# Five Q and K pieces instead of six, and the second V half in one PSUM bank: 32 fewer TensorE instruction pairs a segment

## The chip, the cores and the metric

One core of one Trainium2 chip. The metric is the device time of one execution in microseconds; lower is better. It is about 2 us more than the span from the first to the last instruction that the profile shows. Runs of one kernel can be disturbed and are then marked slow. A ratio in this document is the mean time of one kernel's fast runs over that of the other's of the same rounds, so it is not quite the ratio of the medians quoted beside it. The rule calls a difference under 2% "same".

## The reference, cut to what matters

A recurrent attention over 64 segments, followed by a gated MLP. Each segment takes 32 new rows and 8 memory rows, and its memory output is an input of the next segment, so the 64 segments can't overlap freely.

```python
for s in range(n_seg):                       # 64 segments
    h = jnp.concatenate([mem, xs], axis=1)   # 8 + 32 rows, width 512
    q = jnp.einsum('btd,dhe->bhte', h, Wq)   # 32 heads of 128
    k = jnp.einsum('btd,dhe->bhte', h, Wk)
    v = jnp.einsum('btd,dhe->bhte', h, Wv)
    scores = jnp.where(mask, jnp.einsum('bhqe,bhke->bhqk', q, k) * scale, -1e9)
    o = jnp.einsum('bhqk,bhke->bhqe', _softmax(scores), v)
    o = jnp.einsum('bhte,hed->btd', o, Wo)
    mem = o[:, :M, :]                        # goes into the next segment
```

## The kernel before

The kernel records every operation with what it reads and writes, and works out the semaphore waits itself. The 32 rows of a segment are the stationary operand, 32 columns wide, so four matmuls on four column tiles run side by side ("a quad" below). Work goes in two halves of 16 heads, `b` = 0 and 1. A Q or K piece is `(half, first head pair, head pairs, (bank of Q, bank of K))`; `mi` is 0 for Q, 1 for K.

```python
QKP = ((0, 0, 8, (0, 1)), (1, 0, 4, (6, 7)), (1, 4, 4, (3, 2)))
PVB = (0, 1, 6, 7)                      # banks that PV writes
VB = {(0, 0): 6, (1, 0): 2, (1, 1): 7}  # banks of V

def QK(s, piece, mi):                   # 16 matmuls: 4 quads
    b, p0, np_, banks = piece
    ...
    for dc in range(DC):
        for c in range(4):
            ...
            pe(lambda e, ...: e.matmul(ps[32*c:32*c+32, bank, 0:32*nh], lhsT=hT[:, sl, dc, :], rhs=rhs, ...))

def QK_evac(piece, mi):                 # ACT copies PSUM to Tst, DVE transposes into QT or KT
    ...
def V_evac(b, eng, gs=(0, 4)):          # a copy of V from PSUM to SBUF, on ACT or DVE
    ...
def PV_half(s, b):                      # needs V_sb and the normalised E_sb of half b
    ...

# per segment, cut
for piece in QKP:
    for mi in range(2):
        QK(s, piece, mi)
        QK_evac(piece, mi)
S_half(s, 0); sm_exp(0)
V_half(s, 0, (0, 1, 2))
S_half(s, 1)
sm_sums(0); sm_exp(1); sm_ln(0)
V_half(s, 0, (3,)); V_evac(0, "dve")
V_half(s, 1, gs=(0, 2)); V_evac(1, "dve", (0, 2))     # 16 matmuls of 256 columns, bank 2
sm_sums(1); sm_rcp(0); sm_ln(1); sm_rcp(1)
V_half(s, 1, gs=(2, 4)); V_evac(1, "act", (2, 4))     # 16 of 256 columns, bank 7
sm_norm(0); sm_norm(1)
...                                                   # filler matmuls for later segments, if any
PV_half(s, 0); PV_half(s, 1)
```

Of the kernel before, what the change touches and what calls it, by code (L numbers as in the profile page):

```python
# [169 lines left out]
def fast_path(nc, st, keep, A_x, A_mem0, A_Wq, A_Wk, A_Wv, A_Wo, A_seg_len, B_w_in, B_w_sp, B_b_sp, B_w_out, out):  # L170
# [25 lines left out]
    em = Emitter(n_dma_sems=40)  # L196
# [67 lines left out]
    def PB(b):  # L264
        return ("ps", b)
# [4 lines left out]
    def pe(fn, **k):  # L270
        return em.add("pe", fn, **k)
# [104 lines left out]
    def slot(s):  # L376
        return s % NSLOT
# [74 lines left out]



    QKP = ((0, 0, 8, (0, 1)), (1, 0, 4, (6, 7)), (1, 4, 4, (3, 2)))
    SBK = (0, 1)
    PVB = (0, 1, 6, 7)
    VB = {(0, 0): 6, (1, 0): 2, (1, 1): 7}
# [6 lines left out]
    OC = 384  # L465
    VXB = 5

    def QK(s, piece, mi):
        b, p0, np_, banks = piece
        ws = (w_q, w_k)[mi]  # L470
        bank = banks[mi]
        sl = slot(s)
        h0, nh = 16 * b + 2 * p0, 2 * np_
        for dc in range(DC):
            for c in range(4):
                rhs = ws[:, dc, :].rearrange("p (h c i) -> p c h i", c=4, i=32)[:, c, h0:h0 + nh, :]
                pe(lambda e, dc=dc, c=c, rhs=rhs: e.matmul(ps[32 * c:32 * c + 32, bank, 0:32 * nh], lhsT=hT[:, sl, dc, :], rhs=rhs,  # L477
                                                           start=(dc == 0), stop=(dc == DC - 1), tile_position=(0, 32 * c)),
                   reads=[("hTx", (s // 4) % 3), ("hTm", s), ("W", mi, 2 * b), ("W", mi, 2 * b + 1)], writes=[PB(bank)])

    def halves(b, p0, np_):
        return range(p0 // 4, (p0 + np_) // 4)

    def QK_evac(piece, mi):
        b, p0, np_, banks = piece
        bank = banks[mi]
        st_ = Tst[:, mi, 64 * p0:64 * (p0 + np_)]
        tok = [("T", mi, k) for k in halves(b, p0, np_)]
        act(lambda e: e.activation(out=st_.rearrange("p (hp i r) -> p hp i r", i=32, r=2),  # L489
                                   in_=ps[:, bank, 0:64 * np_].rearrange("p (hp r i) -> p hp i r", r=2, i=32), func=ACT.Copy),  # L490
            reads=[PB(bank)], writes=tok)
        src = st_.bitcast(U32)
        dt_, nm = ((QT, "QT"), (KT, "KT"))[mi]
        dst = dt_[:, b, p0:p0 + np_, :, :].rearrange("p hp q r -> p (hp q r)").bitcast(U32)
        if mi == 0:
            dst = dst.rearrange("p (hp q) -> p hp q", hp=np_)[:, :, 8:40]
        dve(lambda e: e.transpose(out=dst, in_=src), reads=tok, writes=[(nm, b, k) for k in halves(b, p0, np_)])  # L497
# [70 lines left out]
    def V_half(s, b, dcs=range(DC), gs=(0, 4)):  # L568
        bank = VB[b, gs[0] // 2]
        sl = slot(s)  # L570
        w = 128 * (gs[1] - gs[0])
        for dc in dcs:
            for c in range(4):
                c0 = (16 * b + 4 * c + gs[0]) * DH
                pe(lambda e, dc=dc, c=c, c0=c0: e.matmul(ps[32 * c:32 * c + 32, bank, 0:w], lhsT=hT[:, sl, dc, :], rhs=w_v[:, dc, c0:c0 + w],  # L575
                                                         start=(dc == 0), stop=(dc == DC - 1), tile_position=(0, 32 * c)),
                   reads=[("hTx", (s // 4) % 3), ("hTm", s), ("W", 2, 2 * b), ("W", 2, 2 * b + 1)], writes=[PB(bank)])

    def V_evac(b, eng, gs=(0, 4)):
        bank = VB[b, gs[0] // 2]  # L580
        dst, src = V_sb[:, b, 128 * gs[0]:128 * gs[1]], ps[:, bank, 0:128 * (gs[1] - gs[0])]
        tok = [("V", b, g) for g in range(*gs)]
        if eng == "act":
            act(lambda e: e.activation(out=dst, in_=src, func=ACT.Copy, scale=VSC), reads=[PB(bank)], writes=tok)
        else:
            dve(lambda e: e.tensor_scalar(out=dst, in0=src, scalar1=VSC, scalar2=None, op0=ALU.mult), reads=[PB(bank)], writes=tok)  # L586
# [247 lines left out]
    lastop = {}  # L834
    qx_copy(0)
    for s in range(NSEG):
        j4 = s % 4
        rb = s // 4
        if j4 == 1 and rb > 0:
            load_h(rb - 1)  # L840
        if s == NSEG - 1:
            load_h(rb)
        if s % 2 == 1 and s // 2 < NWT:
            wT_piece(s // 2)
        if j4 == 0 and 2 <= rb + 2 < RB:
            load_x(rb + 2, 0)
        if s == 4:
            load_xe(3, 1)

        for piece in QKP:  # L850
            for mi in range(2):
                QK(s, piece, mi)
                lastop["qk"[mi]] = em.by_eng["pe"][-1]
                QK_evac(piece, mi)
        if s == NSEG - 1:
            load_wT(0, [lastop["q"]])
        if s == 0:
            for n in range(2):
                start_v(n)
        S_half(s, 0)  # L860
        sm_exp(0)
        if s == 0:
            for n in range(2, 4):
                start_v(n)
        V_half(s, 0, (0, 1, 2))
        S_half(s, 1)
        lastop["s"] = em.by_eng["pe"][-1]
        sm_sums(0)
        sm_exp(1)
        sm_ln(0)  # L870
        V_half(s, 0, (3,))
        V_evac(0, "dve")
        if s == NSEG - 1:
            sp(lambda e: e.dma_start(w_in1, winr[:, :, 0:FH]), writes=["w_in1"], after=[lastop["s"], lastop["x"]])
            sp(lambda e: e.dma_start(bsp_b, bass.AP(B_b_sp.tensor, B_b_sp.offset, [[0, 128], [1, S]])), writes=["bsp"], after=[lastop["k"]])
            for r in range(8, RB - 2):
                xn2T_dma(r, [lastop["s"], lastop["x"]])
        if s == 0:
            for n in range(4, 8):
                start_v(n)  # L880
        V_half(s, 1, gs=(0, 2))
        V_evac(1, "dve", (0, 2))
        sm_sums(1)
        sm_rcp(0)
        sm_ln(1)
        sm_rcp(1)
        V_half(s, 1, gs=(2, 4))
        lastop["v"] = em.by_eng["pe"][-1]
        V_evac(1, "act", (2, 4))
        sm_norm(0)  # L890
        sm_norm(1)
        if s + 1 < NSEG:
            qx_copy(s + 1)
            lastop["x"] = em.by_eng["pool"][-1]
            lastop["x"] = em.by_eng["pool"][-1]
        if s == 0:
            for j in range(2):
                load_vx(j, "pool")
            for i in range(8, 10):
                start_x(1, i)  # L900
        xs = gx.pop(0) if gx else []
        for f in xs[:2]:
            f()
        PV_half(s, 0)
        PV_half(s, 1)
        for f in xs[2:4]:
            f()
        cT_evac(0, "act")
        cT_evac(2, "dve")
        cT_evac(1, "act")  # L910
        cT_evac(3, "dve")
        for f in xs[4:]:
            f()
        late = []
        Wo((0, 2, 1, 3), OB, 0, OC)
        part_evac(s, OB, 0, OC)
        Wo((0, 2, 1, 3), OB2, OC, D)
        cTx_copy(s)
        part_evac(s, OB2, OC, D)
        if j4 == 3 and rb > 0:  # L920
            F_group(rb - 1, FBK)
            WoX_scatter(rb - 1, FBK)
            h_done(rb - 1, FBK)
        if j4 == 1 and 2 <= rb + 2 < RB:
            ln_inplace(0)
        if s == 5:
            ln_inplace(1)
        if j4 < 2:
            late += gv.pour(2)
        if j4 == 2 and 2 <= rb + 2 < RB:  # L930
            xT(0, FBK)
            late.append(lambda: ring_copy(rb + 2, FBK))
        if s == 9:
            xT(1, FBK)
            late.append(lambda: xe_copy(3, FBK))
        if s + 1 < NSEG:
            mem_out(s)
        if s + 1 < NSEG and s >= 3:
            WoX_mm((s + 1) // 4 - 1, (j4 + 1) % 4)
            if j4 == 2:  # L940
                late.append(lambda: WoX_evac(rb - 1))
        if j4 >= 2:
            late += gv.pour(1)
        for f in late:
            f()
        if s + 2 < NSEG:
            load_vx(s + 2)
        if j4 == 0 and rb >= 2:
            xn2_apply(rb - 2, rb % 2)
            xn2_store(rb - 2, rb % 2)  # L950
        if s == 3 * CK:
            free0 = [done47["s"], done47["x"]]
            sp(lambda e: e.dma_start(w_in2, winr[:, :, FH:F]), writes=["w_in2"], after=free0)
        if 0 <= s - 3 * CK - 1 < 8:
            xn2T_dma(s - 3 * CK - 1, free0)
        if s == 3 * CK - 1:
            done47 = {"s": lastop["s"], "x": px}
        px = lastop.get("x")
# [87 lines left out]
    for rb in range(RB):  # L1046
# [18 lines left out]
        if rb in (2, 3):  # L1065
            r, j, bank = RB - 4 + rb, (rb - 1) % 2, zbank()
# [36 lines left out]
    for tb in range(NTB):  # L1103
        for fb in range(len(ACC) if tb == 0 else 0, FB):
            bank = 5 + fb % 3 if tb == 0 else fb % 2
# [776 lines left out]
```

## Time and profile before

932.83 us, median of three runs (930.78 to 934.89). The profiled run took 925.72 us, less than any of the timed ones.

| what | value |
|---|---|
| span, granted clock | 923.8 us, 0.998 |
| part before the segments; part after the last one begins | 33.3 us; 192.4 us |
| segment without a stall | 10.56 us |
| median of all segments, first QK matmul to the next | 10.75 us |

Of the program's 51,830 instructions 48,083 are TensorE's.

Some groups of the kernel before, one per shape (count, then busy us and mean ns of one):

```profile
L477 PE MATMUL f_ps<-f_arena,f_hT 128*32 128x256 bf16 x4096 | 123.0, 273 | 0.0
L477 PE MATMUL f_ps<-f_arena,f_hT 128*32 128x512 bf16 x2048 | 122.1, 380 | 0.7 <-ACT f_hT L649 0.6
L586 DVE TENSOR_SCALAR f_V_sb<-f_ps 128x256 bf16<-128x256 f32 x64 | 26.6, 415 | 1.3 <-PE f_ps L575 1.1
L584 ACT ACTIVATE f_V_sb<-f_ps 128x256 bf16<-128x256 f32 x64 | 23.4, 366 | 1.8 <-PE f_ps L575 1.8
```

The busy sums say what a quad costs: 2048 matmuls of 512 columns and 4096 of 256, the same columns in all, take 122.1 and 123.0 us. Twice the instructions cost 0.9 us. By start times in the trace a quad of 512 columns takes 216 ns and one of 256 takes 109.

The hole of a late segment without filler (it starts at 720.815 us), in order of time:

```profile
726.30 0.61 PE L575 MATMUL f_ps<-f_arena,f_hT 128*32 128x256 bf16 x16
...
726.93 0.63 DVE L561 TENSOR_TENSOR f_E_sb<-f_R_sb,f_E_sb 128x160 bf16<-128x160 f32 x2
727.11 0.36 ACT L584 ACTIVATE f_V_sb<-f_ps 128x256 bf16<-128x256 f32 x1
727.30 0.38 PEld L594 LDWEIGHTS f_ps<-f_E_sb,f_V_sb 32*128 32x128 bf16 x16 [0.67 <-DVE f_E_sb L561]
727.30 0.49 PE L594 MATMUL f_ps<-f_E_sb,f_V_sb 32*128 32x40 bf16 x16 [0.39 <-DVE f_E_sb L561]
...
727.72 0.28 PE L594 MATMUL f_ps<-f_E_sb,f_V_sb 32*128 32x40 bf16 x16
...
728.09 0.77 ACT L613 ACTIVATE f_cT<-f_ps 128x320 bf16<-128x320 f32 x2 [0.62 <-PE f_ps L600]
```

V's last matmuls (L575) are issued by 726.7; PV's first half (L594) starts at 727.30, its second at 727.72. And one of the stalls with no wait behind it, from the chain of another segment:

```profile
413.36 0.15 PE f_ps L520 x15
413.51 0.04 PE f_ps L526 x4
413.54 0.06 PE f_ps L541
413.60 0.38 issue
413.98 0.21 PE f_ps L541
```

The four matmuls of L541 belong together and only the first waits for anything, yet 0.6 us passes between the first and the second.

### The profile page before, as it was taken

The page shows a single profiled execution, that of the slowest core. Times are in us where ns is not written, and L with a number is a line of the kernel's source. Part 1 is how long each engine was busy: PE and PEld are TensorE (multiplying, and loading weights), DVE is VectorE, ACT ScalarE, POOL GpSimd, SP SyncE. Part 2 cuts the span into 40 slices and gives each one's busy share as a digit, 9 for nine tenths or more (in the row PEclk, how much of TensorE's full clock was granted, in tenths as well). Part 3 has the DMA queues.
Part 4 walks back from the last instruction along what each step waited for, and adds up shares of the span by engine and source line. Part 5 has one row for each costly group of instructions (what it writes and reads, how often), then busy time and mean ns, then how long its engine had stood idle before and what let it go on. Part 6 is the DMA issues. An engine that isn't in the chain of part 4 may idle for free.

```text
span 923.8 us, 51830 instructions
## 1 busy us (share of the span) xinstructions
PE 875.5 (95%) x24038; PEld 572.1 (62%) x24045; DVE 458.0 (50%) x1098; ACT 461.4 (50%) x1281; POOL 155.3 (17%) x408
## 2 busy tenths in 40 slices
PE   6979999999999999999999999899989899999998
PEld 6756667776776777676676777566666544444443
DVE  3434555555554555455555555444445454453433
ACT  2436566666565665556565556555565655400000
POOL 1421111111111111111112111211111122200000
PEclk9999999999999999999999999999999999999999
DMA  9952322122303222222312020413132393021201
GB/s 321 376 154 59 66 52 62 42 50 64 73 19 75 44 56 44 50 61 38 50 44 68 26 78 22 118 27 84 39 55 51 68 269 120 1 98 49 84 12 36
DMA packets 103405, 71.69 MB, mean 78 GB/s; under 512 B 62120, under 2 KB 88688, under 8 KB 103184
## 3 DMA queue, kind: packets, MB, share of 16 engines
q1 hardware_dynamic: 102672, 68.06, 28.2%
q8 instruction: 190, 3.11, 1.5%
q14 instruction: 31, 0.25, 0.1%
q0 software_dynamic: 192, 0.20, 0.1%
q10 hardware_dynamic: 320, 0.07, 0.0%
HBM read 39.46 MB, written 18.61 MB: 63 GB/s over the span
## 4 chain that ended last, share of the span: by engine, by line
PE 89%; DVE 3%; ACT 2%; DMA 2%; issue 2%; SPq 1%; POOL 0%; ACTq 0%
PE f_ps L477 24%; PE f_ps L627 13%; PE f_ps L575 11%; PE f_ps L1025 10%; PE f_ps L404 6%; PE f_ps L594 3%; PE f_ps L671 3%; PE f_ps L423 3%; PE f_ps L987 3%; PE f_ps L1018 3%; PE f_ps L1095 2%; PE f_ps L646 2%; PE f_ps L520 2%; DVE f_V_sb L586 2%; PE f_ps L511 1%
## 5 line engine op out<-in xcount | busy, mean ns | idle before, releaser
L477 PE MATMUL f_ps<-f_arena,f_hT 128*32 128x512 bf16 (+1 forms) x6144 | 233.9, 308 | 0.7 <-ACT f_hT L649 0.6
L477 PEld LDWEIGHTS f_ps<-f_arena,f_hT 128*32 128x32 bf16 x6144 | 160.6, 97 | 77.1 <-ACT f_hT L649 16.6
L489 ACT ACTIVATE f_Tst<-f_ps 128x256 bf16<-128x256 f32 (+1 forms) x384 | 155.7, 453 | 90.0 <-PE f_ps L477 70.9
L575 PE MATMUL f_ps<-f_arena,f_hT 128*32 128x256 bf16 (+1 forms) x3072 | 142.2, 308 | 3.1 <-issue 3.0
L497 DVE STREAM_TRANSPOSE f_QT<-f_Tst 128x128 uint32<-128x128 uint32 (+1 forms) x192 | 65.8, 343 | 155.8 <-ACT f_Tst L489 155.8
L627 PE MATMUL f_ps<-f_arena,f_cT 128*32 128x384 bf16 (+1 forms) x4096 | 125.8, 274 | 9.3 <-ACT f_cT L613 8.7
L627 PEld LDWEIGHTS f_ps<-f_arena,f_cT 128*32 128x32 bf16 x4096 | 85.1, 97 | 52.0 <-ACT f_cT L613 20.9
L565 POOL TENSOR_TENSOR f_E_sb<-f_R_sb,f_E_sb 128x64 bf16<-128x64 f32 x128 | 43.8, 342 | 437.1 <-ACT f_R_sb L557 437.1
L1025 PE MATMUL f_ps<-f_arena 128*128 128x512 bf16 x448 | 101.3, 379 | 2.5 <-DVE f_arena L1031 1.6
L497 DVE STREAM_TRANSPOSE f_KT<-f_Tst 128x128 uint32<-128x128 uint32 (+1 forms) x192 | 68.4, 356 | 46.3 <-ACT f_Tst L489 46.3
L586 DVE TENSOR_SCALAR f_V_sb<-f_ps 128x512 bf16<-128x512 f32 (+1 forms) x128 | 65.9, 553 | 49.1 <-PE f_ps L575 49.0
L639 ACT ACTIVATE f_part<-f_ps 128x384 bf16<-128x384 f32 (+1 forms) x128 | 46.4, 384 | 83.9 <-PE f_ps L627 83.9
L575 PEld LDWEIGHTS f_ps<-f_arena,f_hT 128*32 128x32 bf16 x3072 | 68.7, 96 | 19.5 <-issue 5.1
L615 DVE TENSOR_SCALAR f_cT<-f_ps 128x320 bf16<-128x320 f32 x128 | 56.9, 486 | 47.1 <-PE f_ps L600 47.1
L1025 PEld LDWEIGHTS f_ps<-f_arena 128*128 128x128 bf16 x448 | 43.5, 98 | 56.0 <-DVE f_arena L1031 2.6
L404 PE MATMUL f_ps<-f_hTe,f_arena 128*128 128x128 bf16 x1024 | 72.6, 222 | 1.5 <-DMA f_arena<-in_A_Wk_dram 1.3
L613 ACT ACTIVATE f_cT<-f_ps 128x320 bf16<-128x320 f32 x128 | 49.0, 435 | 48.3 <-PE f_ps L600 48.3
L404 PEld LDWEIGHTS f_ps<-f_hTe,f_arena 128*128 128x128 bf16 x1024 | 58.5, 99 | 12.0 <-issue 10.1
L534 ACT ACTIVATE f_E_sb<-f_ps 128x224 bf16<-128x224 f32 x128 | 45.4, 355 | 35.8 <-PE f_ps L526 34.6
L594 PE MATMUL f_ps<-f_E_sb,f_V_sb 32*128 32x40 bf16 x2048 | 41.5, 178 | 8.9 <-DVE f_E_sb L561 5.7
L1031 DVE TENSOR_TENSOR f_arena<-f_ps,f_arena 128x512 f32<-128x512 f32 x28 | 19.3, 690 | 57.9 <-PE f_ps L1025 57.9
L557 ACT ACTIVATE f_R_sb<-f_R_sb 128x160 f32<-128x160 f32 x128 | 43.1, 337 | 4.4 <-ACT f_part L435 0.4
(103 smaller groups left out, 1052.6 us busy)
## 6 DMA issues: line engine op xcount, KB each, us to landing
wT_d<-f_wst SPq DMA_DIRECT2D x32, 256.0 KB, 3.4
f_arena<-wT_d SPq DMA_DIRECT2D x32, 256.0 KB, 4.6
f_arena<-in_A_Wq_dram SPq DMA_DIRECT2D x4, 1024.0 KB, 9.1
f_arena<-in_A_Wk_dram SPq DMA_DIRECT2D x4, 1024.0 KB, 14.3
f_arena<-in_A_Wv_dram SPq DMA_DIRECT2D x4, 1024.0 KB, 14.9
f_arena<-in_A_Wo_dram SPq DMA_DIRECT2D x4, 1024.0 KB, 13.7
f_Vx<-vext_d SPq DMA_DIRECT2D x62, 64.0 KB, 3.0
vext_d<-f_Vs SPq DMA_DIRECT2D x24, 128.0 KB, 2.2
```

Of the source, the lines that this page charges most:

```text
L404: pe(lambda e, h=h, dc=dc, hh=hh: e.matmul(ps[:, bank, hh * 128:(hh + 1) * 128], lhsT=ws[:, dc, h * DH:(h + 1) * DH], rhs=hTe[:, ck % 3, d ...
L477: pe(lambda e, dc=dc, c=c, rhs=rhs: e.matmul(ps[32 * c:32 * c + 32, bank, 0:32 * nh], lhsT=hT[:, sl, dc, :], rhs=rhs, start=(dc == 0), sto ...
L489: act(lambda e: e.activation(out=st_.rearrange("p (hp i r) -> p hp i r", i=32, r=2), in_=ps[:, bank, 0:64 * np_].rearrange("p (hp r i) -> ...
L497: dve(lambda e: e.transpose(out=dst, in_=src), reads=tok, writes=[(nm, b, k) for k in halves(b, p0, np_)])
L575: pe(lambda e, dc=dc, c=c, c0=c0: e.matmul(ps[32 * c:32 * c + 32, bank, 0:w], lhsT=hT[:, sl, dc, :], rhs=w_v[:, dc, c0:c0 + w], start=(dc ...
L586: dve(lambda e: e.tensor_scalar(out=dst, in0=src, scalar1=VSC, scalar2=None, op0=ALU.mult), reads=[PB(bank)], writes=tok)
L594: pe(lambda e, q=q, c=c, g=g, c0=c0: e.matmul(ps[:, PVB[c], c0:c0 + 40], lhsT=V_sb[q, b, g * 128:(g + 1) * 128], rhs=E_sb[q, b, g * 40:(g ...
L613: act(lambda e: e.activation(out=dst, in_=src, func=ACT.Copy, scale=UNSC), reads=[PB(PVB[c])], writes=[("cT", c)])
L615: dve(lambda e: e.tensor_scalar(out=dst, in0=src, scalar1=UNSC, scalar2=None, op0=ALU.mult), reads=[PB(PVB[c])], writes=[("cT", c)])
L627: pe(lambda e, h=h, g=g, i=i, b=b, c=c: e.matmul(ps[32 * g:32 * g + 32, bank, 0:d1 - d0], lhsT=cTh[:, i, 8:40], rhs=w_o[:, h, d0:d1], star ...
L639: act(lambda e: e.activation(out=part[:, s % 8, d0:d1], in_=ps[:, bank, 0:d1 - d0], func=ACT.Copy), reads=[PB(bank)], writes=[("part", s % ...
L1025: pe(lambda e: e.matmul(ps[:, bank, 0:TB], lhsT=z2[:, sc, fb * 128:(fb + 1) * 128], rhs=wTb[tb % 2][:, :, sc, :], start=(sc == 0), stop=(s ...
```

## The change

The intent: the same columns in fewer, wider matmuls. The 16 heads of Q's second half come in one piece of 512 columns. K's second half stays in two pieces, because its last piece ends the stage and should be short. V's second half goes to one bank and is copied once, by ACT.

```diff
-    QKP = ((0, 0, 8, (0, 1)), (1, 0, 4, (6, 7)), (1, 4, 4, (3, 2)))
+    QKP = ((0, 0, 8, 0, 0), (0, 0, 8, 1, 1), (1, 0, 8, 0, 6), (1, 0, 4, 1, 7), (1, 4, 4, 1, 2))
...
         for piece in QKP:
-            for mi in range(2):
-                QK(s, piece, mi)
-                lastop["qk"[mi]] = em.by_eng["pe"][-1]
-                QK_evac(piece, mi)
+            QK(s, piece)
+            lastop["qk"[piece[3]]] = em.by_eng["pe"][-1]
+            QK_evac(piece)
...
-        V_half(s, 1, gs=(0, 2))
-        V_evac(1, "dve", (0, 2))
+        V_half(s, 1, (0, 1))
         sm_sums(1)
         sm_rcp(0)
         sm_ln(1)
         sm_rcp(1)
-        V_half(s, 1, gs=(2, 4))
+        V_half(s, 1, (2, 3))
         lastop["v"] = em.by_eng["pe"][-1]
-        V_evac(1, "act", (2, 4))
+        V_evac(1, "act")
```

`(0, 1)` and `(2, 3)` are now parts of the contraction, not heads.

More of the change, by code (lines that the diff above doesn't have):

```diff
@@ L466, in fast_path, with QK @@
     VXB = 5
-    def QK(s, piece, mi):
-        b, p0, np_, banks = piece
+    def QK(s, piece):
+        b, p0, np_, mi, bank = piece
         ws = (w_q, w_k)[mi]
-        bank = banks[mi]
         sl = slot(s)
@@ L482, in halves, with QK_evac @@
         return range(p0 // 4, (p0 + np_) // 4)
-    def QK_evac(piece, mi):
-        b, p0, np_, banks = piece
-        bank = banks[mi]
+    def QK_evac(piece):
+        b, p0, np_, mi, bank = piece
         st_ = Tst[:, mi, 64 * p0:64 * (p0 + np_)]
```

## The prediction

> **What bounds the kernel now.** On the page TensorE is busy 95% of the 923.8 us span at a granted clock of 0.998, and the chain that ended last is 89% PE. But the 64 recurrent segments (about 10.75 us each, median, first QK matmul to next) are not dense. In the timeline of a segment late in the run (start 720.8 us; times below count from there) PE is dense only through QK, scores and V, to about 5.9 us; then come two holes: the first PV matmul starts at 6.49, and the output projection at 7.77, after PV and its evacuation. Segments with filler matmuls in these holes last the same (10.56 us without a stall), so a latency chain sets the period there, not the instruction count.
>
> **What the change removes.** Per segment 16 QK pairs and 16 V pairs, the columns staying the same. Four 32-column matmuls run side by side; in the timeline such a quad of N=256 starts 109 ns after the previous one, of N=512 216 ns. So two short quads cost 218, one long 216: 2 ns per merge, 8 merges, about 17 ns a segment, 1.1 us in all. The Trainium skill ("TensorE: Matmul & The Clock Gate", Part 1) gives N/2.4 GHz plus about 2.5 ns start to start; 109 and 216 agree.
>
> **What it moves.**
> - QK: one 512-column ACT copy (597 ns) for two of 256 (about 380 each), one transpose of 445 ns for two of about 290. The last K piece still ends QK, so its copy (3.71), its transpose (to 4.435) and the second score matmuls (4.49) come about 12 ns earlier.
> - V: before, DVE copies the first half (415 ns) and ACT the second (365 ns, 6.29 to 6.66), behind the second reciprocal on ACT. After, ACT copies all 512 in one (597 ns, as the other 512-wide copies), from about 6.275 to 6.87. DVE's first normalisation comes some 0.28 us earlier, so PV of half 0 starts near 6.2 and no longer stalls for the bank that the ACT copy frees (0.2 us now). But PV of half 1 needs that copy: now it starts at 6.905, then at about 6.87 + 0.055 = 6.93.
>
> **Net.** +22 ns a segment on the chain (it already contains the 17 ns saved): about +1.4 us. Against it, PE has some 17 stalls without a semaphore of 0.4 to 1.5 us, about 9 us in all; 64 instructions fewer per segment is 8.5% of PE's instructions, so I estimate -0.8 us. Sum: +0.6 us, about 933.4 us. The runs before spread 4 us.
>
> Chances: faster 0.01, same 0.98, slower 0.01. Range 930 to 937.5 us.
>
> **What would show it.** QK stage 3.473 -> about 3.461 us; V copy a single ACT instruction of about 597 ns; PV half 0 starting near 6.2 where no filler stands, PV half 1 near 6.93, waiting for ACT; period 10.56 -> about 10.58 us; DVE busy down some 35 us, ACT up some 5, neither moving the time.
>
> **What would make it wrong.** A missing-instruction stall that gets rarer or more frequent than in proportion (±3 us); the DVE queue delaying the last K transpose behind the wider Q transpose (+16 ns a segment or more); ACT reaching the V copy earlier than I think, or the second normalisation, not the V copy, deciding PV half 1 (then -17 ns a segment).

## More of the kernel before

The head of the profile page, with its DMA queue of instructions and its chain of work that ended last:

```profile
span 923.8 us, 51830 instructions
PE 875.5 (95%) x24038; PEld 572.1 (62%) x24045; DVE 458.0 (50%) x1098; ACT 461.4 (50%) x1281; POOL 155.3 (17%) x408
...
q8 instruction: 190, 3.11, 1.5%
...
PE 89%; DVE 3%; ACT 2%; DMA 2%; issue 2%; SPq 1%; POOL 0%; ACTq 0%
```

TensorE looks full, but its ends are modelled and its matmuls pipelined. Two things hide in the 95%: short holes in each segment, where PE waits for the softmax, and the "issue" share of 2%, in which the engine waited for nothing that the profile shows. The q8 line gives packets, megabytes and share: 190 blocks of instructions were read during the run.

## The result, and the profile after

921.14 us, median of four runs (919.93 to 921.83), against 933.11 us (930.78 to 934.89): ratio 0.9872, 95% interval 0.9847 to 0.9897. It is below the predicted range of 930 to 937.5 us. In a later session (c1 below) the same pair gave 0.9961 (0.9934 to 0.9989).

The page after:

```profile
span 919.9 us, 47612 instructions
PE 871.6 (95%) x21997; PEld 515.9 (56%) x21997; DVE 432.0 (47%) x970; ACT 474.2 (52%) x1217; POOL 164.1 (18%) x408
...
q8 instruction: 174, 2.85, 1.3%
...
PE 88%; ACT 7%; issue 2%; DMA 1%; DVE 1%; SPq 0%; POOL 0%
```

ACT's share of the chain went from 2% to 7%: work on ACT, the softmax and V's copy, now makes up more of the chain that ended last. The "issue" share is 2% in both. It can't tell the two kernels apart, so the stalls are counted from the traces below. The new copies:

```profile
L476 PE MATMUL f_ps<-f_arena,f_hT 128*32 128x512 bf16 x3072 | 177.6, 380 | 0.7 <-ACT f_hT L647 0.6
L476 PE MATMUL f_ps<-f_arena,f_hT 128*32 128x256 bf16 x2048 | 67.3, 273 | 0.0
L582 ACT ACTIVATE f_V_sb<-f_ps 128x512 bf16<-128x512 f32 x64 | 37.0, 578 | 0.0
```

The hole of a late segment (it starts at 704.164 us):

```profile
710.37 0.27 PE L592 MATMUL f_ps<-f_E_sb,f_V_sb 32*128 32x40 bf16 x16
710.44 0.58 ACT L582 ACTIVATE f_V_sb<-f_ps 128x512 bf16<-128x512 f32 x1
...
711.13 0.20 PEld L592 LDWEIGHTS f_ps<-f_E_sb,f_V_sb 32*128 32x128 bf16 x16 [0.49 <-DVE f_E_sb L559]
711.16 0.28 PE L592 MATMUL f_ps<-f_E_sb,f_V_sb 32*128 32x40 bf16 x16 [0.41 <-ACT f_V_sb L582]
...
711.52 0.77 ACT L611 ACTIVATE f_cT<-f_ps 128x320 bf16<-128x320 f32 x2 [0.50 <-PE f_ps L598]
```

PV's first half is much earlier within the segment (6.21 us after its start; 6.49 before), but its second half later (7.00; 6.905 before), and the second decides. So a segment without a stall became longer, 10.64 us instead of 10.56, and over 63 segments that costs 5 us. The kernel is faster all the same. What went is in the other class of lines:

| | before | after |
|---|---|---|
| stalls without a wait, over 0.33 us, in the segments | 17, 10.8 us | 2, 1.6 us |
| segment without a stall | 10.566 us | 10.641 us |
| part after the last segment begins | 192.4 us | 194.5 us |

(A stall is counted where the next matmul on PE starts over 0.33 us after the one before it, PE was idle in between, and neither that matmul nor what TensorE's sequencer issued just before it carries a wait. The sum is start to start. The "segment without a stall" is the seventh shortest after the first.) The three rows sum to 9.2 less, 63 x 0.075 = 4.7 more and 2.1 more: 2.4 us less, of 3.9 us between the two spans. By stretches the 3.9 us are 0.3 more before the segments, 0.7 less in the first, 5.7 less in the other 62 and 2.1 more after them. The 5.7 us are 4.7 more from the longer segment and 10.3 less of time beyond it. The counted stalls are 7.6 us of the 10.3 (one of the 17, of 1.5 us, lies in the first segment); the rest is shorter stalls and other delays. The 2.1 us contain a spell near 816 us in which the trace shows a granted clock of half: eight matmuls of 512 columns start 425 ns apart instead of 216.

```profile
core 0: us, PE busy (x) PEld busy (x) DVE busy (x) ACT busy (x) POOL busy (x), PEclk, DMA share, GB/s
811.00:814.00 3.00, 1.71 (x8) 0.59 (x6) 1.22 (x2) 0.00 (x0) 0.00 (x0) 1.00 0.13 28
815.00:818.00 3.00, 3.00 (x9) 1.09 (x9) 0.00 (x0) 0.00 (x0) 0.00 (x0) 0.57 1.03 332
```

In the clock records it lasts 3.4 us from 815.4, which by estimate costs up to 1.7 us. It is in the tail, not in what was changed. The traces of e1, e2, e3, c2, d1 and d2 have such a spell between 808 and 837 us too, those of before, a0, c1 and c3 don't; why the clock fell isn't shown.

What the stalls are, the DMA packets of the instruction queue tell. Each of the 17 in before resumed 1.22 to 1.60 us after the end of a 16,384-byte packet of queue q8; so did the two in after (1.36 and 1.43). The stall at 413.37 resumed at 413.98; the packet ran from 411.54 to 412.50. The Trainium skill ("Runtime: NRT & Kernel Launch", Instruction fetch mechanics) says that an engine's instructions are streamed in blocks of 16 KiB, 256 instructions each. The trace agrees: 190 packets for about 48,083 instructions of TensorE, 253 each, and 174 for 43,994, also 253. The page also says that the cost of crossing a block is "mostly hidden". Here it wasn't.

A count settles that the stalls stand at the ends of blocks. Number TensorE's instructions (weight loads, matmuls, semaphore instructions) in the order of their starts in the trace: before the matmul that ends a stall there are always 193 more than a multiple of 256. That holds for all 17 here, for the 2 in after and for all 149 stalls of the eleven traces. A stall that came from a wait would have no reason to keep to one place in 256.

### The profile page after: what moved, and what is told of

It is laid out like the page before. It is cut to its first block, busy times and chain, and to the rows that moved or that the text cites. A ratio compares the mean times of both kernels' runs of the same rounds, so it can differ in the third digit from the quotient of the medians.

```text
span 919.9 us, 47612 instructions
## 1 busy us (share of the span) xinstructions
PE 871.6 (95%) x21997; PEld 515.9 (56%) x21997; DVE 432.0 (47%) x970; ACT 474.2 (52%) x1217; POOL 164.1 (18%) x408
## 4 chain that ended last, share of the span: by engine, by line
PE 88%; ACT 7%; issue 2%; DMA 1%; DVE 1%; SPq 0%; POOL 0%
PE f_ps L476 24%; PE f_ps L625 13%; PE f_ps L1021 11%; PE f_ps L573 9%; PE f_ps L404 7%; PE f_ps L669 3%; PE f_ps L592 3%; PE f_ps L423 3%; PE f_ps L983 3%; PE f_ps L1014 3%; PE f_ps L1091 3%; ACT f_R_sb L555 2%; PE f_ps L518 2%; PE f_ps L644 2%; ACT f_V_sb L582 1%
## 5 line engine op out<-in xcount | busy, mean ns | idle before, releaser
L487 ACT ACTIVATE f_Tst<-f_ps 128x512 bf16<-128x512 f32 (+1 forms) x320 | 156.6, 510 | 88.4 <-PE f_ps L476 87.7
L476 PEld LDWEIGHTS f_ps<-f_arena,f_hT 128*32 128x32 bf16 x5120 | 134.0, 97 | 102.8 <-ACT f_hT L647 15.9
L495 DVE STREAM_TRANSPOSE f_QT<-f_Tst 128x256 uint32<-128x256 uint32 x128 | 57.0, 445 | 179.8 <-ACT f_Tst L487 179.8
L573 PE MATMUL f_ps<-f_arena,f_hT 128*32 128x512 bf16 x2048 | 139.2, 379 | 0.0
L563 POOL TENSOR_TENSOR f_E_sb<-f_R_sb,f_E_sb 128x64 bf16<-128x64 f32 x128 | 52.5, 410 | 420.7 <-ACT f_R_sb L555 420.6
L495 DVE STREAM_TRANSPOSE f_KT<-f_Tst 128x128 uint32<-128x128 uint32 (+1 forms) x192 | 65.6, 342 | 27.7 <-ACT f_Tst L487 26.3
L584 DVE TENSOR_SCALAR f_V_sb<-f_ps 128x512 bf16<-128x512 f32 x64 | 44.3, 691 | 47.0 <-PE f_ps L573 47.0
L592 PE MATMUL f_ps<-f_E_sb,f_V_sb 32*128 32x40 bf16 x2048 | 35.4, 178 | 15.2 <-ACT f_V_sb L582 8.3
L559 DVE TENSOR_TENSOR f_E_sb<-f_R_sb,f_E_sb 128x160 bf16<-128x160 f32 x128 | 41.6, 325 | 16.3 <-ACT f_R_sb L555 16.3
L573 PEld LDWEIGHTS f_ps<-f_arena,f_hT 128*32 128x32 bf16 x2048 | 39.9, 96 | 14.3
```

Source lines behind the costliest of these rows:

```text
L476: pe(lambda e, dc=dc, c=c, rhs=rhs: e.matmul(ps[32 * c:32 * c + 32, bank, 0:32 * nh], lhsT=hT[:, sl, dc, :], rhs=rhs, start=(dc == 0), sto ...
L487: act(lambda e: e.activation(out=st_.rearrange("p (hp i r) -> p hp i r", i=32, r=2), in_=ps[:, bank, 0:64 * np_].rearrange("p (hp r i) -> ...
L495: dve(lambda e: e.transpose(out=dst, in_=src), reads=tok, writes=[(nm, b, k) for k in halves(b, p0, np_)])
L563: pool(lambda e: e.tensor_tensor(out=ev, in0=rv, in1=ev, op=ALU.mult), reads=[("R", b), ("Ex", b)], writes=[("Ex", b)])
L573: pe(lambda e, dc=dc, c=c, c0=c0: e.matmul(ps[32 * c:32 * c + 32, bank, 0:w], lhsT=hT[:, sl, dc, :], rhs=w_v[:, dc, c0:c0 + w], start=(dc ...
L592: pe(lambda e, q=q, c=c, g=g, c0=c0: e.matmul(ps[:, PVB[c], c0:c0 + 40], lhsT=V_sb[q, b, g * 128:(g + 1) * 128], rhs=E_sb[q, b, g * 40:(g ...
```

## The experiments

Theory F (fetch): TensorE's instruction stream runs dry. The change made the bursts of instructions slower, so blocks arrive in time; the longer chain costs 5 us of the gain. Rival, theory D (dependencies): the gain comes from what the change did to waits, that is the relief of DVE, the earlier first half of PV and the bank that comes free earlier.

| run | pairs a segment | segment without a stall, us | stalls | median us | before, same rounds | ratio (95%) |
|---|---|---|---|---|---|---|
| a0 before again | 0 | 10.569 | 13, 9.4 us | 926.6 | 928.21 | 0.9983 (0.994 to 1.0026) |
| e1 Q merge only | -16 | 10.554 | 8, 4.8 us | 918.57 | 928.21 | 0.989 (0.9858 to 0.9922) |
| e2 V merge only | -16 | 10.651 | 2, 1.2 us | 924.59 | 928.21 | 0.9963 (0.9933 to 0.9994) |
| e3 after's waits, before's count | 0 | 10.661 | 20, 16.5 us | 942.0 | 928.21 | 1.0148 (1.011 to 1.0186) |
| c1 after again | -32 | 10.641 | 3, 1.6 us | 923.38 | 927.09 | 0.9961 (0.9934 to 0.9989) |
| c2 after, waits swapped | -32 | 10.554 | 0 | 917.47 | 927.09 | 0.9899 (0.9871 to 0.9928) |
| c3 more instructions still | +32 | 10.771 | 76, 63.8 us | 987.35 (of the three fast runs 979.45) | 927.09 | 1.0569 (1.0517 to 1.0621) |
| d1 = c2 again | -32 | 10.553 | 2, 1.0 us | 915.97 | 923.31 | 0.9914 (0.989 to 0.9938) |
| d2 = e1 again | -16 | 10.555 | 6, 3.8 us | 917.69 | 923.31 | 0.9931 (0.9908 to 0.9955) |

Pairs are counted against before. Stalls and segments are those of the one profiled run of each. All outputs were correct.

### a0: before again

No edit.

> The kernel before, unchanged, for a second trace of it and for the noise. Theory F (fetch): TensorE's own instruction stream (48,000 instructions, read in blocks of 256) runs dry now and then; the trace before has 17 stalls within the segments without a semaphore, about 10.7 us, each resumed 1.2 to 1.6 us after an instruction packet ended. The timed runs of before are some 7 us longer than the traced one, so I expect this trace to show 15 to 40 such stalls, 10 to 20 us in all, 928 to 935 us; ratio to itself 1.00. Theory D (waits: the later V copy and the freed bank and DVE make the gain) says nothing here.

926.6 us (919.1 to 930.21); 13 stalls, 9.4 us. Both are a little under what I expected at least, 928 us and 15 stalls. Each resumed 1.26 to 1.90 us after an instruction packet. So the trace before was typical. Why before ran at 933 us in the first session, 928, 927 and 923 in the others isn't shown by any trace, and stays open. Its runs scatter over 11 us (919.1 to 930.21 here), those of the changed kernel (c1) and of c2 over about 4 us.

### e1 and e2: one half of the change each

e1 is the changed kernel with V as before:

```diff
-        V_half(s, 1, (0, 1))
+        V_half(s, 1, gs=(0, 2))
+        V_evac(1, "dve", (0, 2))
...
-        V_half(s, 1, (2, 3))
+        V_half(s, 1, gs=(2, 4))
-        V_evac(1, "act")
+        V_evac(1, "act", (2, 4))
```

> Only the last Q comes in one 8-head piece; V as in before. 16 TensorE pairs fewer a segment. Theory F: chain of an undisturbed segment 10.56 -> about 10.55 us, stalls fall by half or more: 920 to 927 us. Theory D: nothing that waits on V changes, so within 1 us of before (932 to 934).

918.57 us, 9.6 us under before of the same rounds. The Q merge moves no wait that V or PV sees, the segment without a stall is 12 ns shorter (0.8 us in all), and it has 5 to 9 stalls fewer than the two traces of before. Against the trace of a0 the shorter segment and the fewer stalls make about 5.5 us, and the two traced runs lie 5.1 us apart; the rest of the 9.6 us no trace shows. Theory D had no place for this gain. The expected median, 920 to 927 us, was missed by 1.4 us, with before itself 5 us lower than I assumed.

e2 is the reverse: before with the V lines of the change.

> Only V's second half goes in one bank with one copy on ACT; Q as in before. 16 TensorE pairs fewer. Theory F: undisturbed segment 10.56 -> about 10.65 us (+5.5 us in all), and roughly half of the stalls gone (-8): 928 to 934 us. Theory D: the whole gain is here, about 921 us.

924.59 us, 3.6 us under before. The segment without a stall grew to 10.651 us, as expected from the later copy, and the stalls fell to 2. All of D's causes but the relief of DVE by a wider Q transpose are in this kernel, and of the two halves it gains less.

### e3: the dependencies of after with the instruction count of before

The last Q piece and V's second half are issued as two matmuls of 256 columns into the same bank. Copies, banks, waits and order stay those of the changed kernel.

```diff
+        nsub = 2 if b == 1 and mi == 0 else 1      # in QK; in V_half: 2 if b == 1
+        w = nh // nsub
         for dc in range(DC):
+            for u in range(nsub):
                 for c in range(4):
-                rhs = ws[...][:, c, h0:h0 + nh, :]
-                pe(... e.matmul(ps[32*c:32*c+32, bank, 0:32*nh], ...
+                    rhs = ws[...][:, c, hu:hu + w, :]
+                    pe(... e.matmul(ps[32*c:32*c+32, bank, 32*u*w:32*(u+1)*w], ...
```

> The changed kernel with all its banks, copies and waits, but the last Q and V's second half are issued as two 256-column matmuls into the same bank, so TensorE has as many instructions as before. Theory F: the stalls come back and the longer chain stays (10.65 us a segment): 933 to 940 us, slower than both. Theory D: stays at 921 to 923 us (1.1 us of matmul overhead).

942.0 us, 2 us over the band that theory F gave and far from D's: 14 us slower than before and, over the ratios to before, 2.8% slower than the changed kernel in the first session (1.0148 against 0.9872) and 1.9% in the third. The segment without a stall grew by only 20 ns (8 more quads of 2 ns), so the cost is not in the matmuls; 20 stalls of 16.5 us came, all at the same place in 256 as those of before. This decides for F: same waits, same copies, only the instructions came back. Not all of the 14 us are stalls, though. The mean granted clock of its six timed runs was 0.991, that of before in the same rounds 0.995, which by estimate is up to 4 us; its trace has two spells of 3.4 us at half clock within the segments. The page (the "issue" share of the chain is 2% again):

```profile
span 938.3 us, 51701 instructions
...
PE 87%; ACT 7%; issue 2%; DMA 2%; SPq 1%; DVE 1%; POOL 0%
```

and the two largest "issue" waits of its matmuls, most of it on V's (us in total, times, longest):

```profile
PE f_ps L581 <- issue: 6.1, 8, 1.5
PE f_ps L653 <- issue: 1.5, 2, 0.9
```

Why e3 stalls more than before, with the same number of instructions, is open.

### c1: after again

> The changed kernel again, beside the next two. 917 to 922 us, 0 to 5 stalls of the instruction stream, undisturbed segment 10.64 to 10.65 us without a stall.

923.38 us and 3 stalls; the median is 1.4 us over the expected band. The intervals of the two sessions, 0.9847 to 0.9897 and 0.9934 to 0.9989, don't meet: how much the change gains differs by chip or session. The stalls that the change removes are the part of before that varies, which fits, but is not shown.

### c2: the two waits of PV's second half swapped

The longer chain was larger than forecast (75 ns, not 22). In after ACT's copy ends 6.853 us into the segment and the first matmul of PV's second half starts at 6.999: 146 ns. In before, where PV waited on such a copy alone, it was 56 ns (6.657 to 6.713). That matmul has two waits, and one instruction carries one of them here: the other is a separate semaphore instruction, which took 51 ns after the copy had ended. The late wait was on that one, the early wait (DVE) on the weight load. The edit moves one line of the recording, which changes no engine's order, only which wait comes first:

```diff
         V_half(s, 1, (2, 3))
         lastop["v"] = em.by_eng["pe"][-1]
-        V_evac(1, "act")
         sm_norm(0)
         sm_norm(1)
+        V_evac(1, "act")
```

> The changed kernel with one line moved: the V copy on ACT is recorded after the two normalisations instead of before them. No engine's own order changes; only the two waits of the first matmul of the second PV half swap places, so that the late one (ACT) sits on the weight load and the early one (DVE) on the separate semaphore instruction. If the unforeseen part of the longer chain is that separate instruction behind the late wait (ACT copy ends 6.853, first matmul 6.999, 146 ns; with one wait 56 ns), PV's second half starts 80 to 90 ns earlier, the undisturbed segment falls from 10.65 to about 10.56 us and the time by 5 us, to 913 to 917 us. If the V copy or a bank decides it otherwise, the time stays within 1 us of the changed kernel.

917.47 us, 5.9 us under the changed kernel of the same rounds; the segment without a stall fell from 10.641 to 10.554 us, 63 x 0.087 = 5.5 us. The median is 0.5 us over the expected band, the steps inside the segment are as expected. In the trace the separate instruction, now waiting for DVE, is over at 6.818, before the copy ends at 6.853, and the matmul starts at 6.910. The gap that remains in PV's second half, in a segment that starts at 708.094:

```profile
714.37 0.58 ACT L582 ACTIVATE f_V_sb<-f_ps 128x512 bf16<-128x512 f32 x1
...
715.00 0.17 PEld L592 LDWEIGHTS f_ps<-f_E_sb,f_V_sb 32*128 32x128 bf16 x16 [0.25 <-ACT f_V_sb L582]
```

The wait is now put down to ACT alone, where after showed two, DVE's on the weight load and ACT's on the matmul.

### c3: more instructions still

As e3, but every Q and K piece is issued in 256 columns:

```diff
-        nsub = 2 if b == 1 and mi == 0 else 1
+        nsub = 2 if np_ == 8 else 1
```

> The changed kernel with all its copies, banks and waits, but every 8-head Q and K piece and V's second half issued as 256-column matmuls into one bank: 64 TensorE pairs more a segment than the changed kernel, 32 more than before. Theory F: still more stalls of the instruction stream, 30 to 60 of them, 955 to 975 us. Rival (the first such run was slow for another reason, such as two accumulations in one bank): the cost would be in longer undisturbed segments, not in stalls, and about twice that of the first such run at most by the 2 ns a matmul.

987.35 us, the three fast runs 979.45, with 76 stalls of 63.8 us: more than I expected, in the same direction. Three of its six runs, the profiled one among them, count as slow because they are over 1.5% above its fastest (974.31 us); the profiled run's clock was 0.991. The ratio uses the fast ones. The profile can be read for the kind of its waits all the same:

```profile
PE 85%; issue 6%; ACT 6%; DVE 1%; DMA 1%; POOL 0%; SPq 0%; POOLq 0%
```

"issue" has become as large as ACT. Each of the stalls resumed 1.21 to 1.63 us after an instruction packet, and all 76 stand at the same place in 256. By the ratios the step from after to e3 (32 pairs) costs 1.9 to 2.8% of before, 17 to 26 us, and the step from e3 to c3 (32 pairs more) 4.2%, 39 us: it isn't proportional.

### d1 and d2: the two best, beside each other

No new edits; d1 is c2, d2 is e1.

> The changed kernel with the two waits of PV's second half swapped, again, beside the version with the Q merge alone, on one chip. From the traces: undisturbed segment about 10.56 us, no stall of the instruction stream or one: 914 to 918 us, 1 to 1.5% under before.

> Only the Q merge, again. Undisturbed segment about 10.55 us, but 16 TensorE pairs more a segment than its neighbour, so 5 to 12 stalls, 3 to 7 us: 917 to 922 us, 2 to 5 us over its neighbour. If the stalls did not matter, the two would be equal.

915.97 and 917.69 us. d1 is 0.9914 of before, d2 0.9931. The order is the expected one, but they are 1.7 us apart where 2 to 5 were expected, and the intervals overlap, so they are not clearly apart. d1 had 2 stalls, one more than expected at most, and d2 had 6. Both beat before. c2 also beats the changed kernel on the same chip, clear of its interval.

A version that shares the V copy between DVE and ACT was not run. Whether it or another split helps is open.

## Why the prediction was wrong, point by point

- **The cost of a merge: right.** 2 ns per pair of quads. QK took 3.473 us before and 3.462 after (segments beginning at 265.9 and 264.4 us). The Trainium skill ("TensorE: Matmul & The Clock Gate", Part 1) gives N/2.4 GHz plus about 2.5 ns from start to start; the estimate from it is 215.8 and 109.2 ns, and the trace has 216 and 109.
- **V's copy: right.** One ACT instruction from 6.276 to 6.853 us; 577 ns measured, 597 forecast.
- **PV's first half: right**, 6.205 us ("near 6.2").
- **PV's second half: mechanism right, size off.** "At about 6.87 + 0.055 = 6.93"; it was 6.999. The missing part is the wait on a separate instruction, shown by c2. So the term "+22 ns a segment" measured +75 ns, 4.7 us instead of 1.4.
- **The stalls: this step failed.** "64 instructions fewer per segment is 8.5% of PE's instructions, so I estimate -0.8 us." They were seen, counted and not understood: I scaled them with the number of instructions. They fell from 10.8 us to 1.6, by 85%: 9.2 us where 0.8 was forecast. The prediction did name this among what could make it wrong, but with 3 us. They stand where one block of 256 ends and the next has to be there; that a stall comes when a burst uses a block faster than the next one comes is my reading. I measured in the traces how long 256 TensorE instructions in a row took, within the segments. From the start of the first to that of the last, 11.2% of such stretches took under 3.0 us in before, 4.3% in e1, 3.6% in e2, 11.1% in e3 and none in after and c2 (the shortest: 2.77 us in before, 3.09 in after). But in c3, which stalls most, it is only 3.6%; its stalls themselves lengthen the stretches, and with each stall counted as 50 ns it is 9.3%, still under the 12.0% of before. So this share does not rank the kernels. A packet took 0.88 to 1.83 us and its instructions could run about 1.4 us after its end; that is 2.3 to 3.2 us without the time to ask for it. Merging halves the rate in just the densest parts, from 8 instructions in 109 ns to 8 in 216. A limit near 3 us is thus not shown, and c3 speaks against a single one. That the instruction count makes the stalls, with copies, banks and waits unchanged, is shown by e3.
- **Net.** Forecast +1.4 - 0.8 = +0.6 us. By the traces the terms were +4.7 and -9.2, together -4.5 us. The first session's 12 us between the medians is more than twice that: the timed runs of before there took 5 to 9 us longer than its traced one, and no trace shows why. So the step named above explains the part that the traces hold, and the rest of the miss stays open.
- **Engine sums: half right.** DVE fell by 26 us (35 forecast), ACT rose by 13 (5 forecast). The sums moved nothing; the one copy on ACT that PV's second half waits for did.

## What to carry to other kernels

When a chain of waits shows "issue" stalls on TensorE, look at the DMA queue of instructions: if each stall ends a like time after a packet (1.2 to 1.9 us here), and all stand at one place modulo 256 in the count of TensorE's instructions, the stream of instructions is the limit, and fewer, wider matmuls in the densest stretch can be worth far more than their own few nanoseconds (9.2 us of stalls here, against 1.1 us). Count the stalls in a trace of each version: neither the total of instructions nor the time that 256 in a row take told here how many there would be. And where an instruction has two waits, put the one that comes last directly on it: here this was worth 5.9 us for one moved line.

## What the Trainium skill lacked or had wrong

- "Runtime: NRT & Kernel Launch", Instruction fetch mechanics, calls the crossing of a 16 KiB block "mostly hidden" and gives as the reason an issue floor of about 20 cycles an instruction. On TensorE 8 instructions of a 256-column quad started every 109 ns, 13.6 ns each, and 17 of 190 blocks stalled for 0.4 to 1.5 us (76 of 206 in c3, up to 3.3 us). A sum that a reader could use is missing: a packet of 0.88 to 1.83 us in before, plus 1.2 to 1.9 us over all traces until the stalled instructions ran.
- "TensorE: Matmul & The Clock Gate" counts the cost of a short matmul by columns and a floor of its own. That a stretch of short quads also draws instructions faster than they come is not in it: the 32 pairs of e3 cost 17 to 26 us over the changed kernel, of which the longer segment explains 63 x 20 ns = 1.3 us and its lower granted clock, by estimate, up to 5.
- None of the pages read has the cost of a second wait: 146 ns from the end of the producer to the matmul with the late wait on a separate semaphore instruction, 57 with it on the weight load (6.853 to 6.910 in c2).
